# Four heads of one batch in each unit of the first tile, raw products on 128 columns, and two raw f tiles in the second layer

## The chip, the cores and the metric

The kernel runs on one core of a Trainium2 chip. The metric is the device time of one execution in microseconds (us). Before the change the median of three runs is 641.45 us (641.31 to 641.9).

## What is computed

Three stages follow each other, all in float32. The first is attention over a sliding window of 128 positions with a linear distance bias, for 2 batches, 8 heads, 576 positions and a head dimension of 64. Its output, 1152 tokens of 512, goes through four weighted experts (512 to 1024 to 512, relu), and the result through one more layer pair (512 to 2048 to 512, relu squared).

```python
scores = scale * np.matmul(q, k.transpose(0, 1, 3, 2))
bias = slopes[:, None, None] * (-np.abs(rel).astype(np.float32))[None, :, :]
mask = (rel >= 0) & (rel < window)
scores = np.where(mask, scores + bias[None], -1000000000.0)
scores = scores - np.max(scores, axis=-1, keepdims=True)
attn = np.exp(scores)
attn = attn / (np.sum(attn, axis=-1, keepdims=True) + 1e-09)
x = np.matmul(attn, v)                      # then tokens x (heads * head_dim)
for e in range(E):
    h = np.maximum(x @ w1[e], 0.0)
    out += p[:, e:e + 1] * (h @ w2[e])
h = np.maximum(x @ w_in, 0.0)
y = h * h @ w_out
```

## The kernel before

A float32 product is made on TensorE in one of two ways. Raw: both operands stay float32, and each such matmul shows in the trace as two records. In parts: an operand is rounded to fp32r (`rounded`, on ScalarE or VectorE), the remainder is taken (`rest`, on GpSimd or VectorE), and three fp32r matmuls (high by high, high by low, low by high) replace the product. Raw operands need no preparation by the helpers, parts take three records instead of two.

The 1152 tokens are cut into four chunks for the first expert: chunk 0 has 256 tokens, the first 128 of each batch. The attention runs in units (`units`, `unit_tasks`, `job_tasks`). Four units make the first tile of both batches; before, each holds two heads (pair `c`) of both batches, four squares of 128 x 128 in all. They work raw: scores (L871), a VectorE reduction with bias that also gives the row's extreme (`top`, L917), exponentials on ScalarE with their sums (`exp`, L926), sum and reciprocal (`inv`, L933 and L937), scaling (`norm`, L942), transposition on TensorE (`turn`, L966), a copy to SBUF (`hi`), and probabilities times v (`pv`, L764). `evx` copies the result of a unit, one slice of 128 of x for 256 tokens, to `xfirst`; `xh_later` and `xl_later` make its parts. The other sixteen units work in parts (L879 for the scores, L778 for v).

The first expert is handled in items, one for each chunk and f tile (eight f tiles of 128). The first layer of an item (`item_tasks`, `mm`) multiplies x of the chunk with a weight slice, over four slices k. In chunk 0 the first `RAW1` = 4 f tiles are raw (L1839, one task for each k, 256 columns) and the others in parts (`gemm1_mm`, L1051). The second layer adds h of an f tile into two accumulators of 512 columns, raw for the first `RAW2` = 4 f tiles of chunk 0 (`first_item`, L1790), in parts for the others (`gemm2`, L1287). Weight quarters are loaded raw on SP in the order first layer, second layer, first layer and so on (two f tiles to a quarter, indices 0 to 7 for the first expert). `weight_parts` makes their parts: before, the indices 4 to 7 come first and 0 to 3, whose raw form serves chunk 0, later.

The order of all this is made ahead of time by a list scheduler (`Plan`). Each task has options (engine, time the engine is held, time until the result), a due time, tasks that it depends on, and buffers. `run` takes the task that can start first, and among those of the same engine that can start within 0.15 us of it the one with the earliest due time; it emits the instructions in that order, and each engine then executes its own in that order. So a wrong estimate costs time but no task can overtake another of its engine. Line 129 puts into `gap` how long the engine stood idle in the plan before the task, line 130 moves the engine's time on to the end of the task, and line 135 calls the function that emits it.

`keep_busy` (L554) fills a planned gap of TensorE in the first 24 us with matmuls of zeros (L560), whose number it works out from `plan.gap`. It is called by the scores, by `turn` and by `pv`, not by the products of the items.

The loads for the first tile are made by `first_load` (L1663): one for each of q and k and each half of the heads, with one DMA for each batch in it, on SP except for the first k, which goes by ScalarE's queue; `first_v` (L1671) follows on SP. After 24 items the plan is over and the rest of the kernel is emitted by a loop over items that paces the background work itself.

Of the kernel before, what the change touches and what calls it, by code (L numbers as in the profile page):

```python
# [16 lines left out]
P = 128  # L17
# [125 lines left out]
def kernel(  # L143
# [499 lines left out]
    def unit_tasks(u, due):  # L643
        d = units[u]
        bs, t0, t1, c = d["bs"], d["t0"], d["t1"], d["c"]
        nb = len(bs)
        G = 2 * nb
        q0, q1 = t0 * P, min(t1 * P, S)
# [3 lines left out]


        raw = t0 == 0
        b_ = {k: Buf(k) for k in ("rq", "rk", "rv", "qh", "ql", "khl", "pt", "work")}
# [91 lines left out]
        if t0 == 0:  # L747
            for i in range(nb):
                mm.append((i, P, 0, 2 * i, i * P, P))
        else:  # L750
            for kb in range(t0 - 1, t1):
                tiles = [t for t in (kb, kb + 1) if t0 <= t < t1]
                w = sum(tile_n(t) for t in tiles)
                mm.append((kb - t0 + 1, P, pos, 0, (tiles[0] - t0) * P, w))
                pos += w

        def pv(eng):

            if raw:
                xps = b_["work"].tile = ps_tile("work", [P, nb * nq], "xps")  # L760
                keep_busy(xps[:, 0:P])
                for i in range(nb):
                    for a in range(2):
                        nc.tensor.matmul(  # L764
                            out=xps[a * D:(a + 1) * D, i * P:(i + 1) * P],
                            lhsT=first_in["v"][:, i, (2 * c + a) * D:(2 * c + a + 1) * D],
                            rhs=b_["pt"].tile[:, 2 * i + a, :], start=True, stop=True,
                            skip_group_check=True,
                        )
                if c == NP - 1:  # L770
                    free.extend(first_buf)
# [15 lines left out]
        def evx(eng):  # L787
            if not first_x:
                first_x.append(w_tile([P, KT, CHUNKS0[0][1]], F32, "xfirst"))
            rounded(eng, first_x[0][0][:, c, :], b_["work"].tile)  # L790

        def xh_later(eng):
            rounded(eng, xh[:, c, cols], first_x[0][0][:, c, :])

        def xl_later(eng):
            rest(eng, xl[:, c, cols], first_x[0][0][:, c, :], xh[:, c, cols])
            x_done()
# [22 lines left out]
        if raw:  # L820
            add("evx", [act(nb * nq), dve(nb * nq)], evx, deps=[tpv], bufs=[b_["work"]],
                due=end - 0.9)
            teh = add("evh", [act(nb * nq), dve(nb * nq)], xh_later, shared=True,
                      deps=[task["evx", u]], due=end + 6.0)
            add("evl", [gps(nb * nq), dve(nb * nq)], xl_later, shared=True, deps=[teh],
                due=end + 7.0)
# [6 lines left out]
    def job_tasks(u, i, t, add, b_, end, ready, G, q0, k0, pos, wide):  # L833
# [22 lines left out]
        def scores(eng):  # L856
# [12 lines left out]
            for g in range(G):  # L869
                if raw:  # L870
                    nc.tensor.matmul(  # L871
                        out=sc[0:n, g, :], lhsT=first_in["q", c // 2][0:D, g // 2, 2 * (c % 2) + g % 2, :],
                        rhs=first_in["k", c // 2][0:D, g // 2, 2 * (c % 2) + g % 2, :],
                        start=True, stop=True,
# [26 lines left out]
        def top(eng):  # L901
# [14 lines left out]
            for g in range(G):  # L916
                nc.vector.tensor_tensor_reduce(  # L917
                    out=s["ts"].tile[0:n, g, :], in0=s["sc"].tile[0:n, g, 0:m],
                    in1=bias[0:n, 2 * c + g % 2, off:off + m], scale=QS, scalar=3.0e38,
                    op0=ALU.add, op1=ALU.min, accum_out=s["st"].tile[0:n, 0, g:g + 1],  # L920
# [70 lines left out]

        tb = [task["bias", c, True]] + ([task["bias", c, False]] if t else [])
        if twin:
# [49 lines left out]
    def gemm1_mm(ps, e, ch, f, ks, second=0):  # L1043
# [5 lines left out]
        for k in ks:  # L1049
            for l_, r_ in ((wh, xh), (wh, xl), (wl, xh)):  # L1050
# [604 lines left out]

    def first_load(what, half):
        t, buf = w_tile([P, 2, 4, P], F32, "first")
        first_buf.append(buf)
        first_in[what, half] = t
        src = qT if what == "q" else kT  # L1660
        queue = nc.scalar if (what, half) == ("k", 0) else nc.sync
        for b in range(B):
            queue.dma_start(  # L1663
                out=t[0:D, b], in_=src[b, 4 * half:4 * half + 4, 0:D, 0:P].rearrange("a p s -> p a s")
            )

# [5 lines left out]

    for half in range(2):
        for i, what in enumerate("qk"):
            task["first", what, half] = plan.add(
                "first" + what, [("ACT" if (what, half) == ("k", 0) else "SP", 1.3, 5.2 if half else 4.2)],
                lambda eng, what=what, half=half: first_load(what, half), due=half + 0.1 * i,
            )
# [9 lines left out]

    RAW1, RAW2 = 4, 4

# [116 lines left out]
    def item_tasks(it):  # L1807
# [6 lines left out]

        split = it < 4
        raw = ch == 0 and f < RAW1
        half = it % 2
# [3 lines left out]

        def mm(eng, ks):
            if not split:
                hb["ps"] = ps_tile("work", [P, n], "hps")
            else:
                if ks[0] == 0 and half == 0:
                    wb.tile = ps_tile("y", [P, 2, n], "hps")
                hb["ps"] = wb.tile[:, half, :]
            if ch:
                gemm1_mm(hb["ps"], 0, ch, f, ks, 0)  # L1830
                return
            if KT - 1 in ks:
                x_done()
            if f >= RAW1:
                gemm1_mm(hb["ps"], 0, ch, f, ks, half if split else 0)
                return
            cs = slice((f % FTQ) * P, (f % FTQ + 1) * P)
            for k in ks:
                nc.tensor.matmul(  # L1839
                    out=hb["ps"], lhsT=wtask["raw", wi][:, k, cs], rhs=first_x[0][0][:, k, :],  # L1840
                    start=(k == 0 and not (split and half)), stop=(k == KT - 1),
                    skip_group_check=True,
                )
            if KT - 1 in ks:
                raw_done(wi)
# [4 lines left out]
        t = None if split else itask.get(("g1", it - 1))  # L1850
        for ks in ([[k] for k in range(KT)] if split else [list(range(KT))]):
            t = plan.add(
                f"g1.{it}", [pe(0.00047 * n * (4 if raw else 3) * len(ks))],
                lambda eng, ks=ks: mm(eng, ks),
                deps=w_ready + [
                    task[x, us[k]] for k in ks for x in (("evx",) if raw else ("evh", "evl"))
                ],
                takes=[wb] if ks[0] == 0 and not (split and half) else [],
                bufs=[] if ks[0] == 0 and not (split and half) else [wb],
                due=due, cold=False, follow=[t, itask.get(("k", it - 1, ks[0])) if split else None],  # L1860
            )
            itask["k", it, ks[0]] = t
        itask["g1", it] = t
# [28 lines left out]

        if f == 0 and ch:
            ybufs[ch] = [Buf("y") for _ in range(nt)]
        wi = 2 * (f // FTQ) + 1
        itask["g2", it] = g = plan.add(
            f"g2.{it}", [pe(0.69 * nt)], g2,
            deps=[a, b] + [wtask[p, wi, h] for p in ("hi", "lo") for h in range(2)],
            takes=ybufs[ch] if f == 0 else [], bufs=[b_h] + ([] if f == 0 else ybufs[ch]),
# [130 lines left out]
```

## Time and profile before

| what | value |
|---|---|
| median of three runs | 641.45 us |
| the profiled execution | 641.43 us |
| its span, first to last instruction | 639.7 us |
| TensorE busy | 633.3 us (99%) |
| VectorE, ScalarE, GpSimd busy | 470.3, 299.3, 384.3 us |
| bytes moved | 64.70 MB |

The profile is one execution seen by the hardware profiler; times in it count from the span's start. L560 is line 560 of the kernel before. PE is TensorE's matmuls, PEld its weight loads, DVE is VectorE, ACT is ScalarE, POOL is GpSimd and SP the queue engine. A q behind an engine (SPq) means its DMA issue. An arrow reads output<-inputs, in the names of the program's tiles. Since matmuls overlap, the time of one record is longer than the distance to the next; in a row with x16 the first number is the start, the second the time until the last of the sixteen ends.

### The profile page before, as it was taken

How to read it: one execution, taken by the hardware profiler on the slowest of the kernel's cores; microseconds unless marked ns; L12 is line 12 of the kernel's file. 1: busy time of each engine (PE TensorE's matmuls, PEld its weight loads, DVE VectorE, ACT ScalarE, POOL GpSimd, SP SyncE). 2: the span in 40 equal slices, each digit the busy share in tenths (PEclk: the TensorE clock that was granted, in tenths of full speed). 3: DMA queues.
4: the chain of work that ended last, by engine and by line, in shares of the span. 5: the costliest groups of instructions: out<-in, count | busy, mean ns of one | idle time of the engine just before them, and what ended most of it. 6: DMA issues, size and time to landing. Idle time of an engine off the chain costs nothing.

```text
span 639.7 us, 11060 instructions
## 1 busy us (share of the span) xinstructions
PE 633.3 (99%) x3929; PEld 569.2 (89%) x3929; DVE 470.3 (74%) x1023; ACT 299.3 (47%) x763; POOL 384.3 (60%) x497
## 2 busy tenths in 40 slices
PE   9999999999999999999999999999999999999997
PEld 8778899899898898998998998999999898998996
DVE  6999975378897877777777777768768767667463
ACT  6998765135354344344334334345554544343230
POOL 2589776179667447447447446346687786766531
PEclk9999999999999999999999999999999999999999
DMA  9964330222133444434434434312123223001012
GB/s 233 265 159 104 98 94 26 99 66 99 34 116 115 133 132 127 134 119 141 129 112 157 130 107 127 119 69 67 34 77 124 82 83 116 17 1 51 1 66 83
DMA packets 46983, 64.70 MB, mean 101 GB/s; under 512 B 6480, under 2 KB 29264, under 8 KB 46928
## 3 DMA queue, kind: packets, MB, share of 16 engines
q1 hardware_dynamic: 35520, 39.48, 20.9%
q10 hardware_dynamic: 11408, 24.51, 12.9%
q8 instruction: 31, 0.51, 0.3%
q14 instruction: 24, 0.20, 0.1%
HBM read 53.23 MB, written 10.75 MB: 100 GB/s over the span
## 4 chain that ended last, share of the span: by engine, by line
PE 98%; ACT 1%; DVE 0%; POOL 0%; issue 0%; POOLq 0%
PE yacc L1261 38%; PE hps L1170 35%; PE hps L1051 7%; PE yacc L1287 7%; PE xps L778 2%; PE sc L879 2%; PE tp L966 1%; PE hps L1839 1%; PE yacc L1790 1%; PE sc L560 1%; PE xtp L1353 1%; PE sc L863 1%; ACT ts L926 1%; PE sc L871 0%; PE xps L764 0%; PE ylast L1261 0%
## 5 line engine op out<-in xcount | busy, mean ns | idle before, releaser
L1261 PE MATMUL yacc<-wh,hmem 128*128 128x512 f32 x716 | 228.0, 390 | 0.0
L1261 PEld LDWEIGHTS yacc<-wh,hmem 128*128 128x128 f32 x716 | 134.6, 188 | 27.0
L1261 PE MATMUL yacc<-wl,hmem 128*128 128x512 f32 x358 | 139.9, 391 | 0.0
L536 POOL TENSOR_TENSOR wl<-wraw,wh 128x256 fp32r<-128x256 f32 (+1 forms) x79 | 74.0, 962 | 39.3 <-ACT wh L469 27.7
L536 POOL TENSOR_TENSOR hmem<-c,hmem 128x320 fp32r<-128x320 f32 (+1 forms) x64 | 59.3, 944 | 60.4 <-ACT hmem L1201 60.4
L536 POOL TENSOR_TENSOR ls<-wsum,hs 128x256 fp32r<-128x256 f32 x77 | 61.4, 825 | 54.3 <-ACT hs L414 53.6
L1185 DVE TENSOR_TENSOR u<-hps,p 128x256 f32<-128x256 f32 (+1 forms) x80 | 36.4, 455 | 65.0 <-PE hps L1170 63.1
L1181 ACT ACTIVATE p<-hps 128x256 f32<-128x256 f32 (+1 forms) x80 | 32.8, 410 | 108.8 <-PE hps L1170 108.7
L1261 PEld LDWEIGHTS yacc<-wl,hmem 128*128 128x128 f32 x358 | 67.3, 188 | 12.4
L307 DVE SCALAR_TENSOR_TENSOR wconv<-wraw,wconv 128x512 int32<-128x512 int32 x64 | 58.1, 907 | 1.3
L536 POOL TENSOR_TENSOR la<-wraw,ha 128x256 fp32r<-128x256 f32 x54 | 48.6, 919 | 16.7 <-ACT ha L400 16.7
L1205 ACT ACTIVATE hmem<-c 128x256 fp32r<-128x256 f32 (+1 forms) x72 | 31.3, 445 | 52.8 <-DVE c L1185 51.1
L1206 DVE SCALAR_TENSOR_TENSOR hmem<-c,hmem 128x256 fp32r<-128x256 f32 (+1 forms) x72 | 42.7, 614 | 14.0 <-ACT hmem L1205 13.0
L1201 ACT ACTIVATE hmem<-c 128x320 fp32r<-128x320 f32 (+1 forms) x64 | 27.3, 445 | 52.4 <-DVE c L1195 33.6
L1170 PE MATMUL hps<-ht,ls 128*128 128x320 f32 (+1 forms) x160 | 47.5, 297 | 1.3 <-POOL ls L536 1.3
L1170 PE MATMUL hps<-xh,hs 128*128 128x320 f32 (+1 forms) x160 | 47.7, 298 | 0.0
L1170 PE MATMUL hps<-ht,hs 128*128 128x320 f32 (+1 forms) x160 | 47.6, 297 | 0.0
L1170 PE MATMUL hps<-lt,hs 128*128 128x320 f32 (+1 forms) x160 | 47.4, 296 | 0.0
L1170 PE MATMUL hps<-xl,hs 128*128 128x320 f32 (+1 forms) x160 | 47.4, 296 | 0.0
L1170 PE MATMUL hps<-xh,la 128*128 128x320 f32 (+1 forms) x160 | 47.4, 296 | 0.0
L1170 PE MATMUL hps<-xl,ha 128*128 128x320 f32 (+1 forms) x160 | 47.4, 296 | 0.0
L1170 PE MATMUL hps<-xh,ls 128*128 128x320 f32 (+1 forms) x160 | 47.4, 296 | 0.0
(164 smaller groups left out, 1640.1 us busy)
## 6 DMA issues: line engine op xcount, KB each, us to landing
wraw<-in_w_dram SPq DMA_DIRECT2D x32, 512.0 KB, 3.9
wraw<-in_w_out_dram ACTq DMA_DIRECT2D x16, 512.0 KB, 3.9
w<-wconv ACTq DMA_DIRECT2D x32, 256.0 KB, 4.1
wraw<-w SPq DMA_DIRECT2D x16, 512.0 KB, 3.7
wraw<-in_w_in_dram ACTq DMA_DIRECT2D x14, 512.0 KB, 4.2
rq<-in_qT_dram SPq DMA_DIRECT2D x8, 256.0 KB, 7.7
out_dram<-y SPq DMA_DIRECT2D x7, 256.0 KB, 2.1
rk<-in_kT_dram SPq DMA_DIRECT2D x8, 192.0 KB, 5.6
```

The source lines that it names most:

```text
L307: nc.vector.scalar_tensor_tensor(out=ai, in0=raw[j][:, :, part], scalar=amount, in1=ai, op0=op, op1=ALU.bitwise_or,)
L536: e.tensor_tensor(out=out, in0=in0, in1=f32(in1), op=ALU.subtract)
L778: nc.tensor.matmul(out=xps[a * D:(a + 1) * D, x, o0:o0 + w], lhsT=held["rv"].tile[0:r, k, a * D:(a + 1) * D], rhs=held["pt"].tile[0:r, a, ...
L1051: nc.tensor.matmul(out=ps, lhsT=l_[:, k, cs], rhs=r_[:, k, cols], start=(k == 0 and r_ is xh and l_ is wh and not second), stop=(k == KT - ...
L1170: nc.tensor.matmul(out=ps, lhsT=a[l_][:, k, :], rhs=b[r_][:, k, :], start=start and k == 0 and l_ == r_, stop=stop and k == 1 and l_ == 1, ...
L1181: nc.scalar.activation(out=out, in_=x, func=ACTF.Copy)
L1185: nc.vector.tensor_tensor(out=out, in0=x, in1=y, op=ALU.add)
L1201: nc.scalar.activation(out=hh, in_=r, func=ACTF.Copy)
L1205: nc.scalar.activation(out=hh, in_=src, func=ACTF.Relu)
L1206: nc.vector.scalar_tensor_tensor(out=hl, in0=src, scalar=0.0, in1=f32(hh), op0=ALU.max, op1=ALU.subtract)
L1261: nc.tensor.matmul(out=y, lhsT=l_[:, ns], rhs=r_[:, fo, cols], start=(first and fo == 0 and j == 0), stop=(last and fo == FTQ - 1 and j == 2),
L1287: nc.tensor.matmul(out=y, lhsT=l_[:, ns], rhs=r_[:, fo, :], start=(first and j == 0), stop=(last and j == 2),)
```

## The change

The four units of the first tile become (batch 0, heads 0 to 3), (batch 0, heads 4 to 7), (batch 1, heads 0 to 3), (batch 1, heads 4 to 7); their due times are 6 us apart instead of 2. A unit gives two slices k of x for 128 tokens. The first loads are planned as one task for each batch, in the order batch 0 then batch 1, with new estimates. The raw first layer is cut into one task for each batch and k, 128 columns each. `RAW2` becomes 2: in the second layer of chunk 0 the f tiles 2 and 3 are made in parts, so weight index 3 joins the indices whose parts are made first. `keep_busy` has other numbers in its first branch.

```diff
         early = plan.at["PE"] < 1.0 and plan.gap > 2.0
-        lead, each = (0.6, 0.11) if early else (-0.2, 0.08)
+        lead, each = (-0.9, 0.107) if early else (-0.2, 0.08)
...
-    units = [dict(bs=(0, 1), t0=0, t1=1, c=c, col=0) for c in range(NP)]
+    units = [dict(bs=(b,), t0=0, t1=1, c=c, col=b * P) for b in range(B) for c in range(0, NP, 2)]
...
-            lq, lk, lv = task["first", "q", c // 2], task["first", "k", c // 2], task["first", "v"]
+            lq, lk = (task["first", x, c // 2, bs[0]] for x in "qk")
+            lv = task["first", "v"]
...
-            rounded(eng, first_x[0][0][:, c, :], b_["work"].tile)
+            rounded(eng, first_x[0][0][:, c:c + 2, cols], b_["work"].tile)
...
-        tb = [task["bias", c, True]] + ([task["bias", c, False]] if t else [])
+        tb = [task["bias", c, True]] + [task["bias", c, False] if t else task["bias", c + 1, True]]
...
+    RAW1, RAW2 = 4, 2
+
     hmem = hp.tile([P, 8 * PAIRS[1][1] * 2], F32R, name="hmem")
-    hcount = dict(one=0, two=0)
+    hcount = dict(one=RAW2 % 4, two=0)
...
-    for half in range(2):
-        for i, what in enumerate("qk"):
-            task["first", what, half] = plan.add(
-                "first" + what, [("ACT" if (what, half) == ("k", 0) else "SP", 1.3, 5.2 if half else 4.2)],
-                lambda eng, what=what, half=half: first_load(what, half), due=half + 0.1 * i,
-            )
-    task["first", "v"] = plan.add("firstv", [("SP", 2.4, 4.6)], lambda eng: first_v(), due=4.0)
+    for b in range(B):
+        for half in range(2):
+            for i, what in enumerate("qk"):
+                n = 2 * b + half
+                if (what, half) == ("k", 0):
+                    opts = [("ACT", 0.7, 5.2 if b else 3.9)]
+                else:
+                    opts = [("SP", (1.2, 0.6, 0.6, 0.6)[n], 4.6)]
+                task["first", what, half, b] = plan.add(
+                    "first" + what, opts,
+                    lambda eng, what=what, half=half, b=b: first_load(what, half, b),
+                    due=b + 0.1 * half + 0.01 * i,
+                )
+    task["first", "v"] = plan.add("firstv", [("SP", 2.4, 5.8)], lambda eng: first_v(), due=4.0)
     for u in range(len(units)):
         if u < NP:
-            unit_tasks(u, [14.0 + 2.0 * u])
+            unit_tasks(u, [14.0 + 6.0 * u])
...
-    RAW1, RAW2 = 4, 4
...
+        def mm_raw(eng, b, k):
+            begin = (half, b, k) == (0, 0, 0)
+            if begin:
+                wb.tile = ps_tile("y", [P, 2, n], "hps")
+            hb["ps"] = wb.tile[:, half, :]
+            cs, at = slice((f % FTQ) * P, (f % FTQ + 1) * P), slice(b * P, (b + 1) * P)
+            nc.tensor.matmul(
+                out=hb["ps"][:, at], lhsT=wtask["raw", wi][:, k, cs],
+                rhs=first_x[0][0][:, k, at], start=begin, stop=(k == KT - 1),
+                skip_group_check=True,
+            )
...
+        for i, (b, k) in enumerate((b, k) for b in range(B) for k in range(KT)) if split else ():
             t = plan.add(
+                f"g1.{it}", [pe(0.00047 * P * 4)], lambda eng, b=b, k=k: mm_raw(eng, b, k),
+                deps=w_ready + [task["evx", 2 * b + k // 2]], takes=[wb] if half + i == 0 else [],
+                bufs=[wb] if half + i else [], due=due, cold=False,
+                follow=[t, itask.get(("k", it - 1, i))],
+            )
...
-        if f == 0 and ch:
+        if f == 0 and (ch or not RAW2):
             ybufs[ch] = [Buf("y") for _ in range(nt)]
```

## Rows read from the trace of the kernel before

**Rows 1.** The page: busy time of TensorE, and the chain that ended last.
```profile
PE 633.3 (99%) x3929; PEld 569.2 (89%) x3929; DVE 470.3 (74%) x1023; ACT 299.3 (47%) x763; POOL 384.3 (60%) x497
...
PE 98%; ACT 1%; DVE 0%; POOL 0%; issue 0%; POOLq 0%
```

**Rows 2.** The chain in order of time, 0 to 60: start, duration, what.
```profile
11.38 3.20 ACT ts L926 x16
...
16.27 0.59 PE xps L764 x8
...
39.75 1.72 PE yacc L1790 x4
...
47.91 1.39 PE yacc L1287 x6
```

**Rows 3.** TensorE's instructions in order of time, 0 to 24: start, duration, line.
```profile
1.06 5.62 PE L560 MATMUL sc<-idle 128*128 128x128 bf16 x51 [1.06 <-DVE idle L1635]
6.61 2.08 PE L871 MATMUL sc<-first 64*128 64x128 f32 x16
8.82 1.11 PE L560 MATMUL sc<-idle 128*128 128x128 bf16 x17
9.86 2.05 PE L871 MATMUL sc<-first 64*128 64x128 f32 x16
...
14.63 0.63 PE L966 MATMUL tp<-ident,ts 128*128 128x128 f32 x4 [0.27 <-ACT ts L926]
...
17.28 0.60 PE L1839 MATMUL hps<-xfirst,wraw 128*128 128x256 f32 x2
...
20.91 1.99 PE L1839 MATMUL hps<-xfirst,wraw 128*128 128x256 f32 x8
```

**Rows 4.** Busy time in two stretches: stretch, length, then engine busy (instructions), clock, DMA.
```profile
28.00:44.00 16.00, 16.00 (x108) 12.20 (x107) 14.75 (x45) 15.31 (x48) 13.89 (x19) 1.00 0.75 196
44.00:56.00 12.00, 12.00 (x86) 9.77 (x85) 11.14 (x41) 12.00 (x36) 11.22 (x16) 1.00 0.41 105
```

**Rows 5.** DMA issues around 0.8, then 1.6 us: count, KB, median to landing.
```profile
first<-in_qT_dram SPq DMA_DIRECT2D x1, 128.0 KB, 3.8
first<-in_kT_dram ACTq DMA_DIRECT2D x1, 128.0 KB, 3.1
...
first<-in_qT_dram SPq DMA_DIRECT2D x2, 128.0 KB, 4.2
```

**Rows 6.** VectorE's, then ScalarE's instructions in order of time, 7 to 16.
```profile
7.83 0.29 DVE L917 CUSTOM_DVE_ANT_0 ts<-sc,bias 128x128 f32<-128x128 f32 x1 [3.82 <-PE sc L871]
...
9.85 0.16 DVE L933 TENSOR_REDUCE st<-st 128x4 f32<-128x8 f32 x1
...
10.25 0.69 DVE L942 TENSOR_TENSOR ts<-ts,st 128x512 f32<-128x512 f32 x1
...
8.17 0.40 ACT L926 ACTIVATE ts<-ts,st 128x128 f32<-128x128 f32 x1 [3.34 <-DVE st L917]
...
14.48 0.36 ACT L530 ACTIVATE xfirst<-xps 128x256 f32<-128x256 f32 x1
15.30 0.60 ACT L530 ACTIVATE pt<-tp 128x512 f32<-128x512 f32 x1 [0.46 <-PE tp L966]
```

**Rows 7.** The helpers' instructions in order of time, 29 to 36.
```profile
29.29 0.62 ACT L530 ACTIVATE wh<-wraw 128x512 fp32r<-128x512 f32 x1
...
30.04 0.69 DVE L536 TENSOR_TENSOR wl<-wraw,wh 128x512 fp32r<-128x512 f32 x1
...
35.47 0.42 DVE L1874 SCALAR_TENSOR_TENSOR hmem<-hps,hmem 128x256 fp32r<-128x256 f32 x1
```

**Rows 8.** VectorE's and TensorE's instructions in order of time, around 56.
```profile
55.38 0.68 DVE L536 TENSOR_TENSOR xl<-xps,xh 128x512 fp32r<-128x512 f32 x1
...
56.07 0.28 PE L1051 MATMUL hps<-xh,wh 128*128 128x256 f32 x1
```

**Rows 9.** One line's instructions (L1839): duration in ns, minimum, median, maximum; first, last.
```profile
L1839 PEld LDWEIGHTS hps<-xfirst,wraw x32: 187/190/247, 17.2 to 28.0; 128*128 128x128 f32 x32
```

More of the change, by code (lines that the diff above doesn't have):

```diff
@@ L646, in unit_tasks @@
         nb = len(bs)
-        G = 2 * nb
+        raw = t0 == 0
+        G = 4 if raw else 2 * nb
         q0, q1 = t0 * P, min(t1 * P, S)
@@ L747, in unit_tasks @@
         if t0 == 0:
-            for i in range(nb):
-                mm.append((i, P, 0, 2 * i, i * P, P))
+            mm.append((0, P, 0, 0, 0, P))
         else:
@@ L759, in pv @@
             if raw:
-                xps = b_["work"].tile = ps_tile("work", [P, nb * nq], "xps")
-                keep_busy(xps[:, 0:P])
-                for i in range(nb):
+                xps = b_["work"].tile = ps_tile("work", [P, 2, nq], "xps")
+                keep_busy(xps[:, 0, 0:P])
+                for i in range(2):
                     for a in range(2):
+                        h = 2 * (c + i) + a
                         nc.tensor.matmul(
-                            out=xps[a * D:(a + 1) * D, i * P:(i + 1) * P],
-                            lhsT=first_in["v"][:, i, (2 * c + a) * D:(2 * c + a + 1) * D],
+                            out=xps[a * D:(a + 1) * D, i, :],
+                            lhsT=first_in["v"][:, bs[0], h * D:(h + 1) * D],
                             rhs=b_["pt"].tile[:, 2 * i + a, :], start=True, stop=True,
@@ L769, in pv @@
                         )
-                if c == NP - 1:
+                if u == NP - 1:
                     free.extend(first_buf)
@@ L871, in scores @@
                     nc.tensor.matmul(
-                        out=sc[0:n, g, :], lhsT=first_in["q", c // 2][0:D, g // 2, 2 * (c % 2) + g % 2, :],
-                        rhs=first_in["k", c // 2][0:D, g // 2, 2 * (c % 2) + g % 2, :],
+                        out=sc[0:n, g, :], lhsT=first_in["q", c // 2][0:D, units[u]["bs"][0], g, :],
+                        rhs=first_in["k", c // 2][0:D, units[u]["bs"][0], g, :],
                         start=True, stop=True,
@@ L918, in top @@
                     out=s["ts"].tile[0:n, g, :], in0=s["sc"].tile[0:n, g, 0:m],
-                    in1=bias[0:n, 2 * c + g % 2, off:off + m], scale=QS, scalar=3.0e38,
+                    in1=bias[0:n, 2 * c + g, off:off + m], scale=QS, scalar=3.0e38,
                     op0=ALU.add, op1=ALU.min, accum_out=s["st"].tile[0:n, 0, g:g + 1],
@@ L1654, with first_load @@
     first_in, first_buf, first_x, first_h = {}, [], [], {}
[L1656 to L1659, printed above, removed]
+    def first_load(what, half, b):
+        if b == 0:
+            first_in[what, half], buf = w_tile([P, 2, 4, P], F32, "first")
+            first_buf.append(buf)
         src = qT if what == "q" else kT
         queue = nc.scalar if (what, half) == ("k", 0) else nc.sync
-        for b in range(B):
-            queue.dma_start(
-                out=t[0:D, b], in_=src[b, 4 * half:4 * half + 4, 0:D, 0:P].rearrange("a p s -> p a s")
-            )
+        queue.dma_start(
+            out=first_in[what, half][0:D, b],
+            in_=src[b, 4 * half:4 * half + 4, 0:D, 0:P].rearrange("a p s -> p a s"),
+        )
     def first_v():
@@ L1813, in item_tasks @@
         wi = 2 * (f // FTQ)
-        split = it < 4
-        raw = ch == 0 and f < RAW1
+        split = raw = ch == 0 and f < RAW1
         half = it % 2
@@ L1820, in item_tasks, with mm @@
             itask["bank", it] = wb
[L1822 to L1832, printed above, removed]
-                x_done()
[L1834 to L1844, printed above, removed]
+        def mm(eng):
+            hb["ps"] = ps_tile("work", [P, n], "hps")
+            gemm1_mm(hb["ps"], 0, ch, f, range(KT), 0)
+            if ch == 0:
+                x_done()
+        def mm_raw(eng, b, k):
[8 more added lines that the diff above has]
+                skip_group_check=True,
+            )
+            if (b, k) == (B - 1, KT - 1):
+                x_done()
                 raw_done(wi)
@@ L1850, in item_tasks @@
         t = None if split else itask.get(("g1", it - 1))
-        for ks in ([[k] for k in range(KT)] if split else [list(range(KT))]):
+        for i, (b, k) in enumerate((b, k) for b in range(B) for k in range(KT)) if split else ():
             t = plan.add(
-                f"g1.{it}", [pe(0.00047 * n * (4 if raw else 3) * len(ks))],
-                lambda eng, ks=ks: mm(eng, ks),
+                f"g1.{it}", [pe(0.00047 * P * 4)], lambda eng, b=b, k=k: mm_raw(eng, b, k),
+                deps=w_ready + [task["evx", 2 * b + k // 2]], takes=[wb] if half + i == 0 else [],
+                bufs=[wb] if half + i else [], due=due, cold=False,
+                follow=[t, itask.get(("k", it - 1, i))],
+            )
+            itask["k", it, i] = t
+        if not split:
+            t = plan.add(
+                f"g1.{it}", [pe(0.00047 * n * 3 * KT)], mm,
                 deps=w_ready + [
-                    task[x, us[k]] for k in ks for x in (("evx",) if raw else ("evh", "evl"))
-                ],
-                takes=[wb] if ks[0] == 0 and not (split and half) else [],
-                bufs=[] if ks[0] == 0 and not (split and half) else [wb],
-                due=due, cold=False, follow=[t, itask.get(("k", it - 1, ks[0])) if split else None],
+                    task[x, u] for k in range(KT) for x in ("evh", "evl")
+                    for u in ((us[k],) if ch else us[k // 2::2])
+                ],
+                takes=[wb], due=due, cold=False, follow=[t],
             )
-            itask["k", it, ks[0]] = t
         itask["g1", it] = t
@@ L1891, in g2 @@
             gemm2(0, ch, f, (hb["hh"], hb["hl"]), ys[0, ch], f == 0, f == FT - 1)
-        if f == 0 and ch:
+        if f == 0 and (ch or not RAW2):
             ybufs[ch] = [Buf("y") for _ in range(nt)]
-        wi = 2 * (f // FTQ) + 1
+        wi2 = 2 * (f // FTQ) + 1
         itask["g2", it] = g = plan.add(
             f"g2.{it}", [pe(0.69 * nt)], g2,
-            deps=[a, b] + [wtask[p, wi, h] for p in ("hi", "lo") for h in range(2)],
+            deps=[a, b] + [wtask[p, wi2, h] for p in ("hi", "lo") for h in range(2)],
             takes=ybufs[ch] if f == 0 else [], bufs=[b_h] + ([] if f == 0 else ybufs[ch]),
```

13 lines of the change are left out of this document (6 added, 7 removed).

## Prediction

> **What bounds the kernel now.** The page comes first: TensorE is busy for 633.3 of 639.7 us and 98% of the chain that ended last is its own [rows 1]. A microsecond is therefore worth something only if it is taken out of TensorE's own stream, or out of the time in which that stream holds nothing useful. The chain in order of time shows where the latter lies: up to 16.27 us it passes through filler matmuls (L560: 5.62 and 1.11 us) and through 3.20 us of ScalarE's exponentials, and from there on it is TensorE without a break [rows 2, 3]. The table by stage says who could break it again: from 28 to 56 us TensorE is busy throughout, but ScalarE is busy 27.31 of 28 us, VectorE 25.89 and GpSimd 25.11 [rows 4]. So there are three places to look: the first 17 us (waiting), the raw products and the second layer (TensorE work), and 28 to 56 us, where the helpers are nearly as full as TensorE.
>
> **Part 1: filler ahead of the first scores.** New numbers for `lead` and `each` apply if `plan.at["PE"] < 1.0`. But line 130 has already advanced `at["PE"]` past the scores' start and cost when line 135 calls the function, so the branch is never taken. The trace agrees: (4.28 - 0.2)/0.08 gives 51 fillers, (4.28 + 0.6)/0.11 would give 44, and there are 51 [rows 3]. These numbers do nothing, before or after. What does change is the gap. The planner now believes that the first q lands at 4.6, so the scores start at 4.68 and the same formula gives (4.68 - 0.2)/0.08 = 55 fillers. The 51 take 5.62 us, 0.11 each, which is the spacing of 1.2 GHz at 128 columns; the later 17 take 1.11, 0.065 each at most, near that of 2.4 GHz [rows 3]. Four more are 0.4 us (0.2 if the clock has risen by then), so the first scores move from 6.61 to about 7.0. The data would be there sooner: the first q is issued at 0.80 and lands after 3.8, at 4.6, and the first k lands at 3.9; before, both batches were wanted, and the second q, issued at 1.6, lands after 4.6 (the median of the two is 4.2), at 6.2 [rows 5]. So the smaller first load buys nothing here; its 1.6 us vanish behind fillers. The eight loads stay eight of 128 KB on the same queues, so v and the weights behind them on SP move by nothing that I can see; the second unit's k, third on SP where two issues lie 0.8 apart, goes out near 2.4 and lands near 6.9, before its scores.
>
> **Part 2: the order of the first four units.** I followed the planner's costs and due times (14 + 6u in place of 14 + 2u) by hand up to the first products and then put measured durations on that order. The steps: scores to first VectorE reduction 1.22 (6.61 to 7.83), reduction to first exponential 0.34 (8.17), sixteen exponentials up to 14.48, so 1.58 a unit; sum, reciprocal and scaling 1.1 (9.85 to 10.94); turn to copied result 1.27 (14.63 to 15.90) [rows 3, 6].
> Scores at 7.0, exponentials of unit 0 from 8.56 to 10.1, of unit 1 to 11.7 (seven fillers stand between their scores, which doesn't matter because ScalarE is behind anyway). Unit 0's scaling ends at 11.8, behind unit 1's reduction on VectorE; its turn starts at 11.95, its copy runs on ScalarE from 12.65 to 13.25. The planner puts that copy ahead of unit 2's exponentials, so these run from 13.25 to 14.8. Ten fillers (0.65) fit in before unit 0's probabilities times v at 13.35. The copy of its x waits for ScalarE until 14.8, and the first raw product starts at about 15.3. Two products, unit 1's v product and unit 2's turn follow, and from 16.9 on products are always ready: a batch of one gives 4 x 4 of them. Before, the first product starts at 17.28, after four score units, four turns and two v products [rows 3]. At 0.12 a 128-column record, four score units are 3.84, a turn 0.48 and a v product about 0.45, so useful work ahead of 17.28 is 6.66. After, four scores, three turns, two v products and two raw products (0.48) are also 6.66, and they are done at 16.9. Gain: 0.4 us. Its bounds are -0.4 (the later start of the scores goes all the way through) and 1.9 (the x copy goes ahead of unit 2's exponentials and products start at 13.8 after the v product, of which TensorE can use 1.5 us).
>
> **Part 3: raw products on 128 columns.** Sixteen products of 256 columns (32 records) become 32 of 128 (64 records). Eight records of 256 take 1.99, so (1.99 - 0.38)/7 = 0.23; sixteen of 128 in the scores take 2.05, so (2.05 - 0.27)/15 = 0.12, the transposes (0.63 - 0.27)/3 = 0.12 as well [rows 3]. 64 x 0.12 - 32 x 0.23 = 7.7 - 7.4 = 0.3 us more, bounds 0 (the columns are the same) and 0.7 (0.127 a record).
> The rows leave no room for a weight load at 128 columns: each record has one of its own and they still follow at 0.12. The Trainium skill ("TensorE: Matmul & The Clock Gate", Back-to-back issue gap) speaks against this part: it says that at N=128 the weight load sets the spacing, 81 ns in place of 56. The trace's 17 fillers, each with its load, take 0.065 at most and disagree; by the page's 25 ns the 64 records would cost an estimated 1.6 us more.
>
> **Part 4: the second layer, f tiles 2 and 3.** Raw, one f tile (four records) takes 1.72; in parts, six records take 1.39 [rows 2]. Two f tiles save 2 x 0.33 = 0.66 us, at 39 to 45 us where TensorE has no gap. Bounds 0.6 and 0.7.
> The price is on the helpers: the parts of that weight quarter (two roundings of 0.62, two remainders of 0.69) are wanted by about 40 us instead of after chunk 0, and two remainders of h (0.42 each) are new [rows 7]. That is about 3.5 us on engines of which ScalarE has 0.69 idle, VectorE 2.11 and GpSimd 2.89 between 28 and 56 [rows 4]. What hides it is that TensorE runs ahead there: f tile 7's second layer (1.39) can be brought forward. The next late thing is the xl of the last unit of chunk 1, whose VectorE instruction ends at 56.06 while TensorE starts chunk 1 at 56.07 [rows 8]. I cost it at nothing, bounds 0 and 2.8 us (3.5 + 0.7 arrived early - 1.39).
> The rest has one answer: the second bias that a unit now waits for is built while the fillers run, x copies keep their 256 elements, and `hcount` starting at 2 gives f tile 4 the same place as before. Zero.
>
> **The sum.** -0.4 + 0.3 - 0.66 = -0.76 us. The profiled execution took 641.43 us (span 639.7) and the median is 641.45, so they are alike; forecast 640.7.
>
> **Rivals.**
> *More is gained at the start.* If the x copy runs before unit 2's exponentials, or the clock rises during the fillers (55 at 0.065 would cost 3.6 instead of 5.8), the first product starts about 1 us sooner: 639.7. For: ScalarE's idle stretch from 11.7 to 12.65 in my chain. Against: engines run in program order, and all 51 fillers ran at the slow spacing.
> *The gain is waited away at 56 us.* TensorE arrives 0.76 early, xl comes no earlier: 641.4. For: the 0.01 us of slack there [rows 8]. Against: f tile 7 fills in.
> *Slower: the helpers become the bound before chunk 1.* If the 3.5 us lie on the way to that xl, it comes 3.5 later; 1.39 is covered, 2.1 is not: 643.5. It decides from a delay of 1.39 us on. For: ScalarE's 0.69 us idle [rows 4]. Against: the planner may hand roundings to VectorE and remainders to GpSimd, and part of that work gives way to whatever is due sooner.
> *Slower: weight loads show at 128 columns.* At the 0.19 us that one load takes [rows 9], 64 records take 12.2, 4.8 more than 32 x 0.23: 645.2. Against: every 128-column record in the trace.
> *The lead works after all* (35 fillers or fewer, scores near 5.0): 638.7. Against: the 51.
>
> **How the numbers follow.** Forecast 640.7: 0.50. More gained 0.27, at 639.7, and the working lead 0.02: faster by over 0.2% (below 640.2) 0.29. Waited away 0.09; with the forecast 0.59 within 0.2%. Slower: helpers 0.10, weight loads 0.02, 0.12. About 0.2% (1.3 us) is what a measurement of this kernel can tell from no change. The range runs from 639.3 (part 2 at its far bound) to 642.6 (half of the helpers' price): below lies about 0.08, above 0.11.
>
> **What would show it.** 55 fillers and scores near 7.0 (right), or scores near 5 (wrong); the first raw product at 15 to 16 us; 128-column raw records at 0.11 to 0.12; eight raw second-layer records instead of 16; TensorE unbroken around 56 us and a chunk 1 that starts before 56. A gap there, or filler after 17 us, would make the prediction wrong.

## The result and the profile after

The changed kernel takes 645.40 us (median; 644.58 to 645.71) against 641.47 for the kernel before in the same comparison (641.31 to 641.90): ratio 1.0060, 95% interval 1.0049 to 1.0070. It is 3.9 us slower. The forecast was 640.7 and the range ended at 642.6, so both the sign and the range were wrong. The profiled execution took 645.53, span 643.8. One execution of a later kernel (the second layer with doubled roundings, seven executions) took 2215 us and counts in no ratio here.

The page of the changed kernel, busy time and the chain that ended last (to be read beside [rows 1]):

```profile
PE 633.1 (98%) x3944; PEld 569.4 (88%) x3944; DVE 471.9 (73%) x1025; ACT 298.9 (46%) x760; POOL 385.5 (60%) x500
...
PE 90%; DMA 2%; DVE 2%; ACT 2%; SPq 1%; POOL 1%; issue 1%; ACTq 0%; DVEq 0%; POOLq 0%
```

TensorE works as long as before (633.1 against 633.3) in a span that is 4.1 us longer. What was added is waiting, and the chain, 98% TensorE before, now passes through the helpers and a DMA. The first matmul of line 1170 (1174 after), with which the products over pairs of chunks begin, starts at 152.6 before and 156.8 after, so all of the loss was made before. The waits of TensorE in the changed kernel (engine and line, what it waited for: us in total, times, longest) say for whom:

```profile
PE hps L1174 <- POOL ls L536: 1.3, 1, 1.3
PE tp L968 <- DVE ts L944: 1.1, 1, 1.1
PE sc L560 <- DVE idle L1639: 1.1, 1, 1.1
PE hps L1844 <- DVE hmem L1885: 0.6, 1, 0.6
PE hps L1844 <- ACT xfirst L530: 0.6, 1, 0.6
PE hps L1844 <- ACT hfirst L1784: 0.5, 1, 0.5
PE tp L968 <- ACT ts L951: 0.5, 1, 0.5
PE sc L881 <- DVE khl L536: 0.5, 1, 0.5
```

The kernel before has only the 1.3 and 1.1 that stand here first and third, and two waits of 0.3. The six others are new, come to 3.8 us, and name five different tiles. TensorE's instructions in order of time show where they lie (start, duration, line; in brackets the idle time ahead and who ended it), to be read beside [rows 3]:

```profile
1.06 4.97 PE L560 MATMUL sc<-idle 128*128 128x128 bf16 x55 [1.06 <-DVE idle L1639]
...
14.14 0.71 PE L1844 MATMUL hps<-xfirst,wraw 128*128 128x128 f32 x4 [0.56 <-ACT xfirst L530]
...
16.54 0.63 PE L968 MATMUL tp<-ident,ts 128*128 128x128 f32 x4 [1.10 <-DVE ts L944]
17.01 1.28 PE L1844 MATMUL hps<-xfirst,wraw 128*128 128x128 f32 x10
...
26.42 0.94 PE L1844 MATMUL hps<-xfirst,wraw 128*128 128x128 f32 x6 [0.47 <-ACT hfirst L1784]
...
29.36 0.94 PE L1844 MATMUL hps<-xfirst,wraw 128*128 128x128 f32 x6 [0.60 <-DVE hmem L1885]
...
40.94 0.62 PE L968 MATMUL tp<-ident,ts 128*128 128x128 f32 x2 [0.47 <-ACT ts L951]
...
57.59 0.36 PE L881 MATMUL sc<-khl,qh 128*128 128x256 f32 x1 [0.46 <-DVE khl L536]
```

Idle time alone doesn't add up to the loss, because a group's duration also hides small waits. So I summed the useful records up to an instant, each at the spacing it has where TensorE is never idle (0.112 us for a score, 0.119 for a first-layer record of chunk 1, and so on), and took the sum from the clock. What is left is time without useful TensorE work (us; a single profile for each, good to some 0.4, as the fall from 12.8 to 12.4 shows):

| up to | 16 | 22 | 28 | 32 | 40 | 48 | 58 | 80 |
|---|---|---|---|---|---|---|---|---|
| before | 10.8 | 11.9 | 12.2 | 12.4 | 12.8 | 12.4 | 12.6 | 13.4 |
| after | 10.3 | 11.6 | 13.2 | 14.3 | 14.4 | 15.7 | 17.6 | 17.9 |

Against before, after is ahead by 0.5 at 16 us and by 0.3 at 22, and loses 2.2 between 22 and 32, 1.7 between 40 and 48 and 1.7 between 48 and 58. The table by stage (stretch, length, then busy time of TensorE, weight loads, VectorE, ScalarE, GpSimd) is the surprise. The changed kernel, and under it the first and last stretch of the kernel before:

```profile
16.00:28.00 12.00, 10.76 (x93) 9.78 (x94) 10.45 (x31) 8.08 (x26) 7.10 (x10) 1.00 1.04 257
28.00:44.00 16.00, 14.79 (x100) 11.14 (x100) 14.16 (x42) 13.14 (x41) 11.53 (x17) 1.00 0.68 169
44.00:56.00 12.00, 11.65 (x83) 9.39 (x83) 10.32 (x36) 11.17 (x38) 10.93 (x12) 1.00 0.45 128
56.00:80.00 24.00, 23.54 (x181) 21.42 (x180) 21.71 (x78) 21.39 (x70) 19.79 (x32) 1.00 0.40 103
...
16.00:28.00 12.00, 11.96 (x81) 9.65 (x80) 11.15 (x32) 10.98 (x32) 6.23 (x7) 1.00 1.04 249
...
56.00:80.00 24.00, 24.00 (x193) 21.37 (x192) 21.47 (x76) 18.47 (x62) 20.25 (x30) 1.00 0.41 110
```

Against [rows 4] the helpers are not fuller, they are emptier: ScalarE 13.14 against 15.31 in 28 to 44 us, GpSimd 11.53 against 13.89. They do their work later (56 to 80: 21.39 against 18.47 for ScalarE in the kernel before). Nobody is full. The traces show two ways in which one waits for another: for data, and VectorE beside GpSimd. The k remainder that TensorE waits for at 57.59 took VectorE 1.67 us, where others of its shape take 0.95, while GpSimd made a weight remainder:

```profile
55.77 1.67 DVE L536 TENSOR_TENSOR khl<-rk,khl 64x768 fp32r<-64x768 f32 x1
...
55.36 1.27 POOL L536 TENSOR_TENSOR wl<-wraw,wh 128x512 fp32r<-128x512 f32 x1
```

The DMA in the chain, a load of q that ScalarE waits 1.02 us for at 20.8, is not the cause of the early loss: the next kernel has no such wait and the same TensorE waits up to 28 us (1.1, 0.6, 0.5).

### The profile page after: what moved, and what is told of

It is laid out like the page before. It is cut to its first block, busy times and chain, and to the rows that moved or that the text cites. A ratio compares the mean times of both kernels' runs of the same rounds, so it can differ in the third digit from the quotient of the medians.

```text
span 643.8 us, 11098 instructions
## 1 busy us (share of the span) xinstructions
PE 633.1 (98%) x3944; PEld 569.4 (88%) x3944; DVE 471.9 (73%) x1025; ACT 298.9 (46%) x760; POOL 385.5 (60%) x500
## 4 chain that ended last, share of the span: by engine, by line
PE 90%; DMA 2%; DVE 2%; ACT 2%; SPq 1%; POOL 1%; issue 1%; ACTq 0%; DVEq 0%; POOLq 0%
PE yacc L1265 38%; PE hps L1174 35%; PE yacc L1291 6%; PE hps L1053 6%; DMA rq<-in_qT_dram 2%; PE xps L778 1%; PE sc L881 1%; PE tp L968 1%; SPq L1666 1%; PE xtp L1357 1%; DVE khl L536 1%; PE sc L865 1%; ACT wh L530 1%; DVE wl L536 0%; PE hps L1844 0%
```

## The experiments

The first two take the change apart. The medians of the kernel before differ a little from comparison to comparison (641.35 to 641.68), so each result stands beside its own.

**The units alone** (the change with the second layer left at four raw f tiles):

```diff
-    RAW1, RAW2 = 4, 2
+    RAW1, RAW2 = 4, 4
```

> The changed kernel with RAW2 = 4 again: units, loads and 128-column raw products as changed, the second layer as before. Theory A (the helpers' added work for weight index 3 and the two remainders of h costs the time between 24 and 58 us): the loss goes, the start's gain stays, 641 to 641.7 (the 0.66 us of raw second layer come back). Theory B (the units of one batch, worked through one after the other, leave ScalarE and VectorE waiting between 16 and 32 us, and that time is missing later): 644.5 to 646, ScalarE again busy only about 8 of 12 us between 16 and 28.

Measured: 642.52 against 641.54, ratio 1.0016 (1.0007 to 1.0026). The four-head units cost 1.0 us where the sum had them at -0.1 (-0.4 + 0.3). Neither expectation is met: they are a loss, but a quarter of the whole.

**The second layer alone** (the kernel before with two raw f tiles):

```diff
-    hcount = dict(one=0, two=0)
+    hcount = dict(one=2, two=0)
...
-    RAW1, RAW2 = 4, 4
+    RAW1, RAW2 = 4, 2
...
```

> The kernel before with RAW2 = 2 alone (and the place in hmem that goes with it). Theory A: 643.5 to 645.5, TensorE gaps between 28 and 58 us. Theory B: 640.5 to 641.5, the 0.66 us of TensorE work saved or waited away.

Measured: 644.02 against 641.54, ratio 1.0037 (1.0023 to 1.0052): 2.5 us slower. This is the larger part, and it is small enough to read. TensorE's, VectorE's, then GpSimd's instructions in order of time in this kernel:

```profile
30.02 1.02 PE L1790 MATMUL yacc<-wraw,hfirst 128*128 128x512 f32 x2
32.30 1.12 PE L1790 MATMUL yacc<-wraw,hfirst 128*128 128x512 f32 x2 [1.26 <-DVE hmem L1874]
...
30.14 1.44 DVE L536 TENSOR_TENSOR wl<-wraw,wh 128x512 fp32r<-128x512 f32 x1
31.50 0.42 DVE L897 COPY_PREDICATED sc<-below,sc 128x256 f32<-128x256 uint32 x1
31.84 0.41 DVE L1874 SCALAR_TENSOR_TENSOR hmem<-hps,hmem 128x256 fp32r<-128x256 f32 x1
...
29.27 1.75 POOL L536 TENSOR_TENSOR wl<-wraw,wh 128x512 fp32r<-128x512 f32 x1
```

The second layer of f tile 0 writes two accumulators. Two of its records run at 30.02; the other two, which begin the second accumulator, wait 1.26 us, and not for any data: `yacc` takes a PSUM buffer that still holds the raw h of f tile 2 or 3. A raw f tile's h is copied out of PSUM once, with its relu. An f tile in parts is read twice, by ScalarE for the rounded half (`hh`) and by VectorE for the remainder (`hl`, line 1874), and only the second read gives the buffer back. That read stood on VectorE behind a mask and a weight remainder of 1.44 us, work of the kind that the change itself had brought forward. Elsewhere such a remainder takes 0.69 [rows 7]; the 0.75 more went with another that GpSimd made beside it.

**The second layer alone, with one read.** The theory is then testable: let h of f tiles 2 and 3 leave PSUM in one relu copy, and make both parts from the copy in SBUF.

```diff
...
+        def hc(eng):
+            hb["h"] = first_h[0][0][:, f, :]
+            if eng == "ACT":
+                nc.scalar.activation(out=hb["h"], in_=hb["ps"], func=ACTF.Relu)
...
+            rounded(eng, hb["hh"], hb["h"])
...
+            rest(eng, hb["hl"], hb["h"], hb["hh"])
...
+            c_ = plan.add(f"hc{it}", [act(n), dve(n)], hc, deps=[t], bufs=[wb], due=due + 1.0)
+            a = plan.add(f"hh{it}", [act(n), dve(n)], hh_copy, deps=[c_], takes=[b_h], due=due + 4.0)
+            b = plan.add(f"hl{it}", [gps(n), dve(n)], hl_copy, shared=True, deps=[a], bufs=[b_h], due=due + 4.5)
...
```

Besides the one read the edit makes the parts of h due 3 us later and lets their remainder go to GpSimd and their rounding to VectorE.

> The kernel before with RAW2 = 2 (as in the run with the second layer alone, 644.0), but h of the f tiles 2 and 3 leaves its PSUM bank in one relu copy, as in the raw form, and the parts are made from that copy later (one more copy for each tile, the remainder on GpSimd or VectorE). Theory C (the accumulators wait for the bank of f tiles 2 and 3, and the bank for the second read, VectorE's remainder of h): TensorE's 1.3 us wait for hmem before the first raw second-layer record goes, 642.0 to 643.0. Theory A without the bank (the helpers' work for weight index 3 and h as such): no better, 643.8 to 645.

Measured: 641.55 against 641.35, ratio 1.0002 (0.9992 to 1.0011). All but 0.2 of the 2.5 us is back, though the kernel does two copies more. The first two f tiles' second layer in this kernel, in TensorE's order of time:

```profile
28.69 3.60 PE L1797 MATMUL yacc<-wraw,hfirst 128*128 128x512 f32 x8
```

Eight records in one piece, no wait. That the second read of h held the accumulators' buffer is shown by the wait of 1.26 us and its end here. That the form with one read gives back 2.3 us (2.48 less 0.20) is shown by the two runs. How much of it is the buffer, and how much the later due times and the other engines, is not shown.

**The whole change, with one read** (the same edit in the changed kernel):

> The whole change with the same one-read copy of h. Theory C: 1 to 2 us below the change, 643.4 to 644.4. Without it: 645 to 646.

Measured: 644.41 against 641.35, ratio 1.0045 (1.0029 to 1.0062): 3.1 us over before instead of 3.9. In the whole change one read gives back only 0.9, and the two intervals overlap, so even that is not clear of noise. There the second read held up a first-layer product (0.60 at 29.36, in the view above) rather than an accumulator.

**Weight parts early, nothing else** (the kernel before, all four f tiles raw, but the parts of that weight quarter made first, ahead of chunk 0's items and of the indices 4 to 7, instead of behind them):

```diff
-        later = T0 + (T1 if raw else 0.0) + ITEM * (FTQ * g + (LAG if k else 0))
+        later = T0 + (T1 if raw and i != 3 else 0.0) + ITEM * (FTQ * g + (LAG if k else 0))
...
-    parted = sorted(range(PER), key=lambda i: (FTQ * order[i][1] < (RAW1, RAW2)[order[i][2]], i))
+    parted = sorted(range(PER), key=lambda i: (i != 3 and FTQ * order[i][1] < (RAW1, RAW2)[order[i][2]], i))
...
```

> The kernel before, whole second layer of four f tiles raw, but the parts of weight index 3 are made first, as in the change, and not after chunk 0. It adds no work, it only moves two roundings and two remainders from after 56 us to about 30 us. Theory A (helpers full): 642.5 to 643.5. Theory C alone: 641.3 to 642.0, since no bank waits for a remainder.

Measured: 642.09 against 641.35, ratio 1.0013 (1.0003 to 1.0022). That lies between the two expectations. Moving two roundings and two remainders forward costs 0.7 us; TensorE has no single long wait for it. With it the second layer with one read adds up: -0.66 (fewer records) + 0.74 (parts early) = +0.1, measured +0.2. (The 2.3 is the difference of the two runs with the second layer alone, so that it leads from there to their 2.5 proves nothing.)

**The due times of the units** (the change with the old step between them):

```diff
-            unit_tasks(u, [14.0 + 6.0 * u])
+            unit_tasks(u, [14.0 + 2.0 * u])
```

> The changed kernel with the due times of the first four units 2 us apart again, so that these units run side by side and not one after the other. Theory A: no better than the change, 644.5 to 646. Theory B, in the form that the order of the units is the cause: 641 to 643, with ScalarE busy over 10 of 12 us between 16 and 28.

Measured: 645.41 against 641.54, ratio 1.0059 (1.0044 to 1.0074), the same as the change, though the first raw product starts at 17.93 here and at 14.14 there. The due step is not the cause.

**The q remainder later** (units alone; GpSimd's first remainder of q is held back until VectorE has scaled the third unit's exponentials). In the changed kernel, VectorE's scaling and GpSimd's remainder, in order of time:

```profile
11.83 0.69 DVE L944 TENSOR_TENSOR ts<-ts,st 128x512 f32<-128x512 f32 x1
...
14.76 1.64 DVE L944 TENSOR_TENSOR ts<-ts,st 128x512 f32<-128x512 f32 x1
...
14.58 1.27 POOL L536 TENSOR_TENSOR ql<-rq,qh 128x512 fp32r<-128x512 f32 x1 [8.19 <-DVE st L935]
```

The same instruction takes 0.69 alone and 1.64 beside GpSimd's, 0.95 more, and it ends 0.55 after GpSimd's does, less than one scaling. Before, GpSimd was not busy at all between 8 and 16 us. The Trainium skill ("SBUF — State Buffer", SBUF: two separate sides) says that a VectorE instruction with two SBUF inputs and a GpSimd instruction that reads SBUF share one pair of ports, and that whichever starts first holds it for its whole length. The two rows agree with that but for 0.14 us: GpSimd's started 0.18 earlier, and VectorE's ended 0.55 after it, where a whole scaling takes 0.69.

```diff
-            tql = add("ql", [gps(G * nq), dve(G * nq)], ql, shared=True, deps=[tqh], takes=[b_["ql"]],
+            tql = add("ql", [gps(G * nq), dve(G * nq)], ql, shared=True,
+                      deps=[tqh] + [task["j0no", 2]] * (u == NP), takes=[b_["ql"]],
```

> Units, loads and 128-column products as changed, RAW2 = 4 (642.5 in that form); GpSimd's first remainder of q is held back until VectorE's scaling of unit 2 is done. Theory D (GpSimd and VectorE in each other's way: that scaling took 1.64 us beside GpSimd, 0.69 alone, and TensorE waited 1.1 us for it): scaling at 0.69, no wait at 16 us, 641.3 to 642.0. If the time is lost later anyway: 642.3 to 643.

Measured: 642.66 against 641.35, ratio 1.0019 (1.0010 to 1.0028); the units alone had 1.0016. The scaling's collision and the 1.10 us wait at 16 us are gone: TensorE's stalls between 13 and 30 us in this kernel are only

```profile
13.90 0.71 PE L1845 MATMUL hps<-xfirst,wraw 128*128 128x128 f32 x4 [0.56 <-ACT xfirst L530]
...
16.50 0.71 PE L1845 MATMUL hps<-xfirst,wraw 128*128 128x128 f32 x4 [0.27 <-ACT xfirst L530]
...
28.35 0.36 PE L882 MATMUL sc<-khl,qh 128*128 128x256 f32 x1 [0.80 <-DVE khl L536]
```

and time without useful work up to 22 us falls from 11.4 (units alone) to 10.5. The median doesn't fall: it is 1.3 over its own before, where the units alone were 1.0 over (by the intervals, a gain of up to about half a microsecond can't be excluded). At 28.35 there is a new wait of 0.80 for a k remainder. But the trace doesn't show the gain being handed back there: it is of the fastest of the ten executions, 641.85, which is 0.9 less than the profiled one of the units alone (642.73). So the medians show that this wait at 16 us is not the whole of what the units cost, and where the microsecond goes stays open.

**A lag of the helpers, made on purpose.** By 28 us the units alone leave VectorE, ScalarE and GpSimd 2.7 us of work behind (16 to 28 us: 25.6 busy against 28.4). To see what such a lag costs in the old order, four roundings on ScalarE are written twice, in the kernel before and in the second layer alone with one read:

```diff
             rounded(eng, b_["qh"].tile, b_["rq"].tile)
+            if eng == "ACT" and NP <= u < NP + 2:
+                rounded(eng, b_["qh"].tile, b_["rq"].tile)
...
             rounded(eng, b_["khl"].tile[0:D], b_["rk"].tile)
+            if eng == "ACT" and NP <= u < NP + 3:
+                rounded(eng, b_["khl"].tile[0:D], b_["rk"].tile)
```

> Kernel before with four roundings on ScalarE written twice (the k of the first three units of the second group, 0.83 us each, the q of one, 0.61), so that some 2.8 us of useless work lie on ScalarE between 16 and 25 us. By 28 us the units' order left ScalarE, VectorE and GpSimd together 2.7 us of work behind the kernel before (25.6 against 28.4 busy). Theory A, this lag is what the units alone cost: 642.2 to 643. Theory B, it is the order of the particular waits in the units and not the lag, so that ScalarE's slack takes the double work in: 641.3 to 641.9.

> The same double roundings in the kernel with the second layer on two raw f tiles and one read of h (641.55 without them). Theory A, the lag of the helpers meets the weight parts and remainders that the second layer wants by 40 us, and this is the interplay that leaves the whole change with one read at 644.4: 643.8 to 645. Theory B, the lag is not the cause: at most the same step as in the kernel before with double roundings, 641.5 to 642.6.

Measured: 643.85 against 641.68, ratio 1.0032 (1.0019 to 1.0045), and 643.91 against 641.68, ratio 1.0033 (1.0021 to 1.0045). Busy time by stage of the first of the two:

```profile
16.00:28.00 12.00, 10.28 (x65) 8.10 (x64) 8.94 (x27) 11.84 (x33) 3.97 (x6) 1.00 1.02 252
```

The doubled roundings took 3.3 us, and the time grew by 2.2: ScalarE, busy for 10.98 of these 12 us in the kernel before, had no room for them. The experiment overshot: without the 3.3 the three helpers were busy for 21.5 us from 16 to 28, 6.9 less than before (0.9 of it they had done by 16, since the scores began at 5.59 in this execution, the fastest of the six at 642.63). VectorE and GpSimd stood behind ScalarE. So it shows that helper work there costs TensorE time, but it is no copy of the units' 2.7. On the interplay, 643.91 lies in the range of theory A, but only because the doubled roundings cost 2.2 in the kernel before too. Theory A wanted a larger step in the second kernel: the step is 2.2 without the second layer's change and 2.0 with it (2.23, less the 0.20 of that kernel without doubles).

**Fewer fillers** (the change with its lead in force):

```diff
-        early = plan.at["PE"] < 1.0 and plan.gap > 2.0
+        early = plan.gap > 4.0
```

> The changed kernel with a condition under which the new lead numbers apply (a planned gap over 4 us), so 35 fillers stand ahead of the first scores instead of 55. If an earlier start reaches the end: about 1 us faster than the change, 644.4. If the helpers decide from 22 us on (A and B alike): within 0.4 us of the change, 645.0 to 645.8, with the first scores near 5 us.

Measured: 647.69 against 641.54, ratio 1.0094 (1.0079 to 1.0109): 2.3 us slower than the change, and neither expectation is met. TensorE's instructions in order of time, then the table by stage, whose last three columns begin with the granted clock (1.00 is 2.4 GHz, 0.50 is 1.2):

```profile
1.06 3.58 PE L560 MATMUL sc<-idle 128*128 128x128 bf16 x35 [1.06 <-DVE idle L1639]
4.74 1.13 PE L873 MATMUL sc<-first 64*128 64x128 f32 x8
5.80 0.56 PE L560 MATMUL sc<-idle 128*128 128x128 bf16 x7
7.18 3.40 PE L873 MATMUL sc<-first 64*128 64x128 f32 x16 [0.81 <-DMA first<-in_kT_dram]
...
6.00:8.00 2.00, 1.19 (x12) 1.04 (x10) 0.84 (x8) 1.65 (x8) 0.40 (x2) 0.89 1.21 190
8.00:16.00 8.00, 8.00 (x45) 6.76 (x44) 4.93 (x31) 3.66 (x17) 1.27 (x1) 0.50 1.07 313
16.00:18.00 2.00, 2.00 (x12) 1.79 (x12) 1.04 (x3) 1.35 (x6) 0.00 (x0) 0.55 1.14 275
```

The scores do start at 4.74. But the second unit's k isn't there; TensorE stands 0.81 us at 6.4, and from 8 to 16 us it is granted 1.2 GHz. First raw product: 16.91, against 14.14 in the change. That is one profiled execution. The mean granted clocks of the four executions (0.992, 0.999, 0.999, 0.996) don't go with their times (647.47, 648.10, 647.92, 646.76), so that the clock makes the 2.3 is likely from this trace and not shown.

## Why the prediction was wrong

**Part 1 held, but for the clock.** 55 fillers, as worked out; the new `lead` and `each` are never used. They took 4.97 us instead of 6.0, because the clock rose at 4.7, among them; before, all 51 ran slow. So the scores began at 5.95, not 7.0. That is luck of this execution: in other kernels with 55 fillers the clock rose at 4.2, 4.6, 5.0 and 7.0, and nothing in the trace of before told it. The last of these is the change with one read. There all fillers ran slow, and scores and first raw product began where the prediction had them, at 7.0 and about 15.3:

```profile
7.04 1.16 PE L873 MATMUL sc<-first 64*128 64x128 f32 x8
...
15.23 0.71 PE L1850 MATMUL hps<-xfirst,wraw 128*128 128x128 f32 x4 [0.56 <-ACT xfirst L530]
```
The rival in which the lead works (638.7) failed both ways: the lead isn't used, and made to work it costs 2.3.

**Part 2 held up to 16 us and failed after.** The first raw product came at 14.14, ahead of the forecast 15.3 by about as much as the early clock gave. The sentence that failed is "from 16.9 on products are always ready". The next turn waited 1.10 us for a scaling that ran beside GpSimd, which I had taken at its duration from [rows 6]; and I followed the helpers only as far as that first product. Behind it ScalarE is busy for only 8.08 us between 16 and 28 (10.98 before). A gain of 0.4 was forecast; the units alone cost 1.0, part 3's 0.3 among it. I priced TensorE's order and not the helpers'.

**Part 3 held.** Ten records took 1.28, (1.28 - 0.27)/9 = 0.112 each; 64 x 0.112 = 7.2 us. Records of 256 columns follow each other at 0.216 where TensorE doesn't wait, 6.9 us for 32, so the cut costs the 0.3 of the sum. The weight loads don't show, as the traces of before said.

**Part 4's saving held, its price didn't.** Eight raw second-layer records instead of sixteen, 0.66 us. "I cost it at nothing" is the step that failed most. For the second layer alone the price was 3.1 (2.48 slower, and the 0.66 saved), at or above even the upper bound of 2.8: 0.74 for the early parts, 2.3 for h in two reads, and 0.1 left over. In the whole change it was 3.6 (3.93 less the units' 0.98, and the 0.66). The working treated the two h remainders as 0.42 us of VectorE each. What they cost is where they stand in the queue and what they hold: a PSUM buffer that the accumulators take. The cover, f tile 7's second layer, was of no use, because TensorE's order is written out beforehand and it waited at 31 us with that work far behind in its queue. (The range's end of 642.6, called half of this price, is 642.1 by that working; it changes nothing here.)

**The rivals.** "The helpers become the bound" had the sign (643.5, chance 0.10) and not the mechanism: the helpers are less busy, the xl at 56 isn't waited for, and most of the loss is made before 48 us. "More is gained at the start" came true at 14 us, by the clock, and the time still rose. I gave faster 0.29 and slower 0.12 with [rows 4] in hand, in which three helpers are 90% to 98% busy; the reading that TensorE "runs ahead" there was assumed, not read.

**The sum, by the runs.** The two halves, as they were built, add up: 0.98 (units) + 2.48 (second layer) = 3.5 of 3.9, and the 0.5 left is within the intervals. What doesn't add up is the form with one read: 0.98 + 0.20 = 1.2, measured 3.1 (644.41; by its interval 1.9 to 4.0). In pieces: -0.66 (records) + 0.74 (parts early) + 0.98 (units) + 0.87 (two reads, in the whole change) = +1.9, of +3.9. The other 2.0 appear only when both halves are together, also with one read. That kernel's waits are again short and on different things (0.8 in two waits for k remainders, 0.6, 0.5, 0.5), with a loss between 46 and 58 us. A plain lag of the helpers doesn't reproduce it. Its cause stays open; that two orders of helper work disturb each other is only an argument. One candidate stands in the traces and was not tested. Between 14 and 58 us VectorE's subtractions of two SBUF tiles and its scalings took 3.9 us more than the shortest of their shape before, 5.3 in the units alone, 5.7 in the second layer alone, 7.1 in the change and 6.3 with one read, and in these five traces each that took over 0.4 more overlaps a subtraction on GpSimd. It can't be the whole: the run with the old due times has 5.1 and the time of the change. No version was found that beats the kernel before; the second layer with one read equals it.

## What to carry to other kernels

When an operation is split in parts, ask not only what each part costs but which buffer its last reader gives back, and what stands ahead of that reader on its engine; one copy out of PSUM, and parts made from the copy, cost two more instructions and, in the second layer alone, saved 2.3 us. Where helpers are 90% busy and TensorE's order is fixed, microseconds of helper work, moved or added, come out in the time (0.7 and 2.2 here), and a gain ahead of such a stage need not reach the end: a wait of 1.1 us that was taken out left the median where it was. Price a change of order by following every engine to the end of the stage, not to the first matmul that comes sooner.

## What was not expected of the hardware

In one execution a stall of 0.81 us at the start was followed by more than 8 us at 1.2 GHz (granted clock 0.50 from 8 to 16 us); that kernel, with 20 fillers fewer and its scores 1.2 us earlier, was 2.3 us slower. One VectorE scaling went from 0.69 to 1.64 us beside a GpSimd subtraction. And the clock's first rise moved from execution to execution, though TensorE ran fillers without a gap from 1.06 us on: it came at 4.2, 4.6, 4.7, 5.0 and 7.0 us in five kernels that begin with the same 55 fillers, and at 3.9 to 6.8 in six that begin with the same 51. In the three of these eleven profiled executions with the earliest rise, 3.9 (second layer with one read), 4.2 (q remainder later) and 4.4 us (doubled roundings in the kernel before), the time is the lowest of all executions of its kernel (641.05, 641.85 and 642.63, against medians of 641.55, 642.66 and 643.85). So part of the spread between executions seems to be made there, and one trace need not be like the median's execution.
